# A new order for a planned attention and convolution kernel: other due times, other engines for some eighty steps

## The chip, the cores and the metric

The kernel runs on one core of a Trainium2 chip. A core has TensorE (PE; its weight loads are counted apart as PEld), VectorE (DVE), ScalarE (ACT), GpSimd (POOL) and SyncE (SP), which here only starts DMAs; 16 DMA engines serve all its queues. The metric is the device time of one execution in microseconds (us). The three runs of the kernel before took 371.64, 371.68 and 374.29, so the median is 371.68.

## The reference

Four batches of eight heads, 768 positions, 64 channels a head. First comes attention in which a query sees only the keys of its own cluster:

```python
q_assign = np.argmax(np.einsum('bhsd,hcd->bhsc', q_n, c_n), axis=-1)   # 16 centroids a head
k_assign = np.argmax(np.einsum('bhsd,hcd->bhsc', k_n, c_n), axis=-1)
mask = q_assign[:, :, :, None] == k_assign[:, :, None, :]
scores = np.where(mask, scale * np.matmul(q, k.transpose(0, 1, 3, 2)), -1000000000.0)
attn = softmax(scores)
out = np.matmul(attn, v)
```

The eight heads of a batch are put side by side to 512 columns, x, and a gated long convolution follows:

```python
proj = x @ w_proj                                  # 512 -> 3 * 512: x1, x2, x3
X2 = np.fft.rfft(x2, n=S, axis=1)
H = np.fft.rfft(filter_fft, n=S, axis=0)[None, :, :]
y = x1 * np.fft.irfft(X2 * H, n=S, axis=1) * x3
return (y @ w_out).astype(np.float32)
```

## The kernel before, in words

**Units.** The work is cut into eight groups `n` (half a batch, four heads each), and each group into two pairs of heads. For a pair, `attention` (line 683 on) runs over six tiles of 128 keys. For each tile there are three score products of 512 columns (`sc`, line 700), three exponentials on ACT into a buffer `p` (lines 714 and 717), the product p·V (`pv`, line 728, 96 of them in all, numbered 1 to 96 in this document), and the sum of the p for the softmax's denominator: the first two tiles are added by DVE or POOL (line 737), the other four by DVE (line 741). There are five buffers `p`.

**Masks.** A query and a key of different clusters must give a score far below the others. Keys and queries carry 16 more rows for that beside their 64 channels in the tiles `aug`: the one-hot of the cluster, for queries scaled and shifted. `routing` (line 589 on) makes them for a group: products with the centroids (`L647`), a transposition and an argmax on DVE (`L652` to `L662`), two products with a triangular matrix that pick the first of equal maxima (`bank<-ohB,tri`, one for each half of the positions), two small steps for each of them on ACT or DVE that write `ohT` (`L673` or `L675`), and then eight DMAs of 24 KB (`aug<-ohT`, line 512), which put the rows where the score products read them.

**Loads.** Queries, keys and V come by DMA from SP's queue (lines 324, 331, 337, 343). Keys of the later groups come in four pieces and are transposed by DVE (`L605`), queries are transposed by PE (`L627`). A load can begin when the step that last read its buffer is done. There are four buffers for queries and keys and three for V. The filter (line 432, into `y`) and the weights (lines 1097 and 1101, POOL's queue) are loaded once.

**Denominators.** For most pairs the sum over partitions is made by DMAs: three accumulating moves from POOL's queue (`acc<-acc`, line 774), a move to DRAM (`dd<-acc`, line 778), and from there back, a reduction and a reciprocal on DVE (`dn`, `L787`), and two broadcasting loads (`rb<-dr`, line 791). For the first two and the last groups PE makes it with a product with ones (`L754`) and one copy (`den`, `L760` or `L762`).

**Convolution.** When both groups of a batch are done, `hyena` runs beside the attention of the next: products with w_proj (`L855` for x2; the gate products `bank<-xT,wpj` for x1 and x3), forward transform, products with the filter's spectrum `hm` on DVE (`L885`), inverse transform (`bank<-inv,y`), folding (`L956`, `L966`), gating (`L929`, `L971`) and the product with w_out.

**What sets the order.** No order of instructions is written down. Every step is recorded with `op`, line 95: the engines that may run it with a cost for each, its reads and writes, and a due time. `place`, line 124, then runs a list planner on these costs: whenever an engine is free, it takes, among the steps that can start within 0.1, the one with the smallest due time, and for a step with several engines the engine that can start it first. Loads (`kind="load"`) don't start before their due time, on SP's queue as on POOL's. The steps are then issued in the order of their planned starts, and each engine runs its own part of that list in order; SP and POOL, too, do not pass a DMA that waits. Two tables adjust the planner, both keyed by the running number of the step:

```python
o.due += NUDGE.get(o.seq, 0.0)
```

```python
if o.seq in ONLY:
    o.eng = {ONLY[o.seq]: o.eng[ONLY[o.seq]]}
```

`NUDGE` (line 43) has an entry for each of the 1983 steps and is added to its due time. `ONLY` (line 44) fixes the engine of some steps. PE has two more details: a product of 128 output rows is issued as one instruction when the array stands in its mode of 128 columns and as two of 64 columns otherwise (`product`, line 80), and score products and gate products take the mode that they find.

Of the kernel before, what the change touches and what calls it, by code (L numbers as in the profile page):

```python
# [87 lines left out]
class Plan:  # L88
# [6 lines left out]
    def op(self, eng, fn, due, r=(), w=(), alloc=None, free=(), lock=False, byts=0, after=(), kind=None, lat=0.0, tab=None):  # L95
# [3 lines left out]
        o.seq = len(self.ops)  # L99
        o.due += NUDGE.get(o.seq, 0.0)  # L100
        o.outs, o.end, o.start, o.on = [], None, None, None
# [22 lines left out]
    def place(self, free0, banks_for, switch=0.1, wait=0.1, rate=RATE, bonus=0.0, margin=0.02195, shape=0.0):  # L124
# [58 lines left out]
        for o in self.ops:  # L183
            if o.seq in ONLY:
                o.eng = {ONLY[o.seq]: o.eng[ONLY[o.seq]]}
        for o in self.ops:
# [1109 lines left out]
```

## Time and profile before

| | us |
|---|---|
| median of three runs | 371.68 |
| the profiled execution | 372.84 |
| its span | 371.1 |
| PE busy in the span | 354.5 |
| DVE busy | 337.6 |
| ACT busy | 264.3 |
| POOL busy | 121.5 |

The span is from the first to the last instruction in the profile; 1.74 us of the execution's time lie around it. PE's busy time holds matmuls only, and their ends are modelled. The longest groups are the 768 instructions of p·V with 142.7 us and the exponentials with 109.1 and 57.9 us; DVE spends 111.9 us in the sums of line 741. Where a view names what an engine waited for, it takes the last of the semaphores that the instruction waited on.

### The profile page before, as it was taken

The page shows a single profiled execution, that of the slowest core. Times are in us where ns is not written, and L with a number is a line of the kernel's source. Part 1 is how long each engine was busy: PE and PEld are TensorE (multiplying, and loading weights), DVE is VectorE, ACT ScalarE, POOL GpSimd, SP SyncE. Part 2 cuts the span into 40 slices and gives each one's busy share as a digit, 9 for nine tenths or more (in the row PEclk, how much of TensorE's full clock was granted, in tenths as well). Part 3 has the DMA queues.
Part 4 walks back from the last instruction along what each step waited for, and adds up shares of the span by engine and source line. Part 5 has one row for each costly group of instructions (what it writes and reads, how often), then busy time and mean ns, then how long its engine had stood idle before and what let it go on. Part 6 is the DMA issues. An engine that isn't in the chain of part 4 may idle for free.

```text
span 371.1 us, 8436 instructions
## 1 busy us (share of the span) xinstructions
PE 354.5 (96%) x3191; PEld 202.5 (55%) x3191; DVE 337.6 (91%) x449; ACT 264.3 (71%) x502; POOL 121.5 (33%) x152
## 2 busy tenths in 40 slices
PE   7999989999999999999989999968999999999995
PEld 4555445444555554654546545545466766566662
DVE  6988887999999879999998999998998999989993
ACT  7999977876977686797798673758965787323433
POOL 7452442300035447123100057425021432134610
PEclk9999999999999999999999999999999999999999
DMA  7879897364599866769667958673367650110214
GB/s 173 214 147 202 174 175 168 76 136 76 120 182 171 139 118 100 118 149 140 119 85 167 241 108 127 146 137 41 88 97 184 147 76 0 47 45 2 116 57 172
DMA packets 109797, 46.20 MB, mean 124 GB/s; under 512 B 97640, under 2 KB 103484, under 8 KB 109756
## 3 DMA queue, kind: packets, MB, share of 16 engines
q1 hardware_dynamic: 105772, 36.05, 43.1%
q0 software_dynamic: 2752, 8.98, 17.1%
q10 hardware_dynamic: 1232, 0.62, 0.6%
q8 instruction: 25, 0.41, 0.5%
q14 instruction: 16, 0.13, 0.1%
HBM read 31.59 MB, written 7.40 MB: 105 GB/s over the span
## 4 chain that ended last, share of the span: by engine, by line
PE 56%; DVE 21%; ACT 6%; DMA 6%; issue 5%; POOL 2%; SPq 2%; DVEq 0%; ACTq 0%; POOLq 0%
PE bank L85 23%; PE pair L728 23%; DVE acc L741 5%; DMA qkraw<-in_k_dram 2%; PE bank L855 2%; DVE xT L820 2%; PE bank L83 2%; PE bank L627 2%; PE bank L647 2%; DVE sd L956 2%; DVE tm L869 1%; DMA aug<-ohT 1%; DVE acc L737 1%; DMA dd<-acc 1%; DVE yy L966 1%
## 5 line engine op out<-in xcount | busy, mean ns | idle before, releaser
L728 PE MATMUL pair<-p,vraw 128*64 128x385 f32 x768 | 142.7, 488 | 0.8 <-ACT p L717 0.8
L717 ACT ACTIVATE p<-bank 128x512 f32<-128x512 f32 x192 | 109.1, 612 | 19.0 <-PE bank L85 10.7
L741 DVE TENSOR_TENSOR acc<-p,acc 128x1536 f32<-128x1536 f32 x64 | 111.9, 1749 | 4.3 <-POOL acc L737 1.6
L728 PEld LDWEIGHTS pair<-p,vraw 128*64 128x64 f32 x768 | 56.2, 136 | 45.9 <-issue 38.1
L85 PE MATMUL bank<-aug,aug 80*64 80x256 bf16 (+3 forms) x682 | 75.5, 327 | 4.2 <-DMA aug<-ohT 1.4
L85 PEld LDWEIGHTS <-aug 80*64 80x64 bf16 (+1 forms) x682 | 42.4, 109 | 41.4 <-issue 29.6
L714 ACT ACTIVATE p<-bank 128x512 f32<-128x512 f32 x96 | 57.9, 607 | 7.5 <-PE bank L85 6.2
L774 POOL DMA_DIRECT2D acc<-acc x30 | 24.0, 819 | 102.5 <-DVE acc L741 46.6
L85 PE MATMUL bank<-xT,wpj 128*64 128x384 bf16 x488 | 44.8, 326 | 1.2 <-ACT ohT L673 1.1
L285 POOL CAST aug<-qkP 64x768 bf16<-64x768 f32 x26 | 21.3, 823 | 66.1 <-DVE acc L741 23.3
L85 PEld LDWEIGHTS <-wpj 128*64 128x64 bf16 x488 | 30.3, 110 | 13.3 <-issue 4.3
L85 PEld LDWEIGHTS <-y 128*64 128x64 bf16 x456 | 23.9, 110 | 14.6 <-issue 5.1
L885 DVE TENSOR_TENSOR tm<-bank,hm 128x512 f32<-128x512 f32 x44 | 28.5, 682 | 3.0 <-PE bank L490 2.0
L85 PE MATMUL bank<-wout,y 128*64 128x512 bf16 (+1 forms) x200 | 24.2, 372 | 1.3 <-DVE y L971 0.9
L889 POOL TENSOR_TENSOR y<-tm 128x512 bf16<-128x512 f32 x16 | 20.2, 1274 | 14.0 <-DVE tm L885 7.7
L737 POOL TENSOR_TENSOR acc<-p,p 128x1536 f32<-128x1536 f32 x6 | 20.7, 3458 | 8.7 <-DVE uv L874 4.4
L283 ACT COPY qkP<-bank 128x384 f32<-128x384 f32 x35 | 15.8, 480 | 10.0 <-PE bank L85 4.6
L855 PE MATMUL bank<-wpj,xT 128*64 128x512 bf16 x192 | 22.0, 379 | 0.2 <-DVE xT L820 0.2
L283 ACT COPY ob<-bank 128x512 f32<-128x512 f32 x22 | 12.4, 594 | 13.4 <-PE bank L85 9.9
L283 ACT CAST aug<-qkP 64x768 bf16<-64x768 f32 x25 | 20.5, 829 | 0.4
L737 DVE TENSOR_TENSOR acc<-p,p 128x1536 f32<-128x1536 f32 x10 | 17.7, 1765 | 2.9 <-ACT p L714 1.4
L627 PE MATMUL bank<-ident,qkraw 128*128 128x128 f32 x120 | 18.6, 281 | 0.8 <-DMA qkraw<-in_k_dram 0.8
(176 smaller groups left out, 443.1 us busy)
## 6 DMA issues: line engine op xcount, KB each, us to landing
qkraw<-in_q_dram SPq DMA_DIRECT2D x30, 192.0 KB, 3.4
rb<-dr SPq DMA_DIRECT2D x30, 192.0 KB, 3.3
qkraw<-in_k_dram SPq DMA_DIRECT2D x50, 96.0 KB, 2.8
vraw<-in_v_dram SPq DMA_DIRECT2D x48, 96.0 KB, 3.1
out_dram<-ob SPq DMA_DIRECT2D x9, 512.0 KB, 3.1
acc<-acc POOLq DMA_DIRECT2D x10, 384.0 KB, 5.1
acc<-acc POOLq DMA_DIRECT2D x10, 192.0 KB, 4.2
vraw<-in_v_dram SPq DMA_DIRECT2D x4, 384.0 KB, 4.3
```

The costliest lines, as they stand in the source:

```text
L85: T.nc.tensor.matmul(out[64 * i:64 * i + 64], lhsT[:, 64 * i:64 * i + 64], rhs, start=start, stop=stop)
L283: T.nc.scalar.copy(out, in_)
L285: (T.nc.vector if e == "DVE" else T.nc.gpsimd).tensor_copy(out, in_)
L627: T.nc.tensor.transpose(ap(h)[:, ts(t, 128)], raw(s, 3 * ch + t), T.ident[:, ::-1] if ch > j else T.ident)
L714: T.nc.scalar.activation(o, ap(h).rearrange("p (a b) -> p a b", a=2), Act.Exp, scale=0.125)
L717: T.nc.scalar.activation(flat(s)[:, lo:lo + 512], ap(h), Act.Exp, scale=0.125)
L728: T.nc.tensor.matmul(o[64 * hp:64 * hp + 64, ch, :385], T.vraw[vs][:, hp, sk * D:(sk + 1) * D], T.p[slots[sk]][:, hp, 384 * ch:384 * ch + ...
L737: alu(e).tensor_tensor(T.acc[os], T.p[slots[0]][:, :, :S], T.p[slots[1]][:, :, :S], op=Alu.add)
L741: T.nc.vector.tensor_tensor(T.acc[os], T.p[slots[sk]][:, :, :S], T.acc[os], op=Alu.add)
L774: op(("POOL", .8), lambda e, rows=rows: T.nc.gpsimd.dma_start(flat_()[:rows], flat_()[rows:2 * rows], accum_op=Alu.add), te, r=[], w=AK, b ...
L855: T.nc.tensor.matmul(ap(h)[64 * i:64 * i + 64], T.xT[xs][:, kt, c:c + 64], T.wpj[:, kt, DM:2 * DM], start=kt == 0, stop=kt == ND - 1)
L885: op(("DVE", .68), lambda e, i=i, cs=cs, r=r, h=h: T.nc.vector.tensor_tensor(T.tm[r][:, cs], ap(h), hmrow(i, (0, 2, 2, 3)[2 * r + cs]), op ...
```

## The change

Only the two tables change. All 1983 entries of `NUDGE` are new numbers. `ONLY` has 102 entries where it had 113. Cut to entries that are spoken of, each on a line of its own:

```diff
-NUDGE = {
+NUDGE = {
...
-128:-20.837, 129:-31.203, 130:-22.135, 131:21.705,        # filter loads
+128:13.22, 129:12.796, 130:-10.311, 131:10.695,
...
-266:-49.0695, 267:15.6865, 268:11.6885, 269:13.0825,      # four pieces of keys, group 2, first pair
+266:-4.39, 267:4.93, 268:0.957, 269:8.02,
...
-684:-14.97122,                                            # dd<-acc, group 2, first pair
+684:-2.473,
...
-1196:-842.80587, 1197:-916.07187, 1198:-711.43587, 1199:-834.24287,   # masks, group 5
+1196:-19.574, 1197:-42.2, 1198:-17.755, 1199:-21.803,
...
-1338:8.27978, 1339:16.77478, 1340:12.95378, 1341:6.79878, # four pieces of V, group 6, first pair
+1338:-8.792, 1339:-8.067, 1340:-9.3, 1341:-2.232,
...
-1366:-212.95227, 1369:-4591.25327,                        # bank<-ohB,tri of group 6, two halves
+1366:0.062, 1369:1.656,
...
...
-ONLY = {
+ONLY = {
...
-72:"ACT", 149:"ACT", 224:"POOL", 231:"POOL", 252:"ACT", 255:"ACT",
+72:"DVE", 149:"DVE", 155:"DVE", 176:"DVE", 224:"DVE", 231:"DVE", 252:"DVE", 255:"DVE",
...
```

A due time says nothing by itself: it counts against those of the other steps that are ready. What comes out in the order of the instructions is this. PE has the same 634 groups of products, in nearly the same order for score products and p·V; the others move by some places against them. 15 score products instead of 32 find the array in the mode of 128 columns, so PE has 2284 matmuls instead of 2267 to issue, for the same columns. Of the 48 loads of V pieces 29 stand earlier against PE's work and 16 later, 8 groups of products earlier in the mean; of the 48 of key pieces 35 earlier and 9 later, 4 groups in the mean. The 60 mask moves stand as before in the mean, 29 earlier and 24 later. The V pieces of group 6's first pair are issued when products 64 to 67 stand next to them in the list, before 70 to 72; they are first needed by product 73. Of the key pieces of group 2's first pair three stand 14, 11 and 3 groups earlier, one 5 later.

Some eighty steps change their engine. Counted by engine, DVE has one cast to `aug` more, two output copies, two scalings `tm<-bank,hw` (line 468) and two denominators more, one step `L405` and one copy to `fw` more, one `ohT` and two copies `x` more, three copies to `qkP`, one `od` and one `L966` less. ACT has the most of these the other way and three casts and three `qkP` copies more. POOL has four casts and one fill less and one fold more. Of the first sums p + p (line 737) that of group 0's first pair goes from POOL to DVE and that of group 1's second pair from DVE to POOL. On DVE, two of the products into `hm` stand ahead of the first transposition of keys, where all stood behind it.

More of the change, by code (lines that the diff above doesn't have):

```diff
@@ new lines @@
+ONLY = {15:"POOL",16:"ACT",17:"POOL",30:"ACT",32:"SP",33:"SP",34:"SP",35:"SP",37:"SP",38:"SP",40:"SP",67:"ACT",69:"DVE",72:"DVE",73:"DVE",86:"DVE",91:"DVE",100:"POOL",101:"POOL",147:"ACT",149:"DVE",155:"DVE",159:"DVE",161:"DVE",176:"DVE",224:"DVE",225:"POOL",230:"DVE",231:"DVE",236:"POOL",237:"DVE",243:"DVE",251:"DVE",252:"DVE",254:"ACT",255:"DVE",325:"ACT",408:"POOL",411:"POOL",418:"POOL",420:"ACT",421:"POOL",503:"ACT",526:"ACT",531:"DVE",532:"DVE",533:"POOL",563:"DVE",571:"POOL",600:"DVE",701:"POOL",703:"POOL",706:"ACT",708:"ACT",710:"POOL",712:"DVE",873:"DVE",876:"ACT",879:"ACT",880:"POOL",884:"DVE",889:"POOL",901:"DVE",1033:"DVE",1042:"DVE",1071:"DVE",1072:"POOL",1085:"POOL",1087:"DVE",1096:"ACT",1099:"ACT",1167:"DVE",1169:"ACT",1171:"POOL",1174:"POOL",1179:"ACT",1183:"POOL",1355:"ACT",1356:"POOL",1358:"POOL",1461:"DVE",1489:"POOL",1529:"ACT",1533:"DVE",1537:"ACT",1555:"POOL",1641:"ACT",1644:"POOL",1649:"ACT",1650:"ACT",1843:"DVE",1911:"POOL",1919:"ACT",1960:"SP",1963:"SP",1966:"ACT",1969:"DVE",1970:"SP",1974:"SP",1977:"ACT",1978:"ACT",1981:"ACT"}
```

3 lines of the change are left out of this document (1 added, 2 removed).

## The prediction

> **What bounds the kernel now.** I read the busy shares first, then the same in stretches, then the waits of PE, then the instructions in order of time where PE stood still.
>
> ```profile
> PE 354.5 (96%) x3191; PEld 202.5 (55%) x3191; DVE 337.6 (91%) x449; ACT 264.3 (71%) x502; POOL 121.5 (33%) x152
> ...
> 0.00:10.00 10.00, 8.12 (x39) 4.60 (x39) 6.90 (x25) 7.44 (x12) 7.17 (x40) 1.00 0.74 167
> 10.00:25.00 15.00, 13.86 (x128) 7.67 (x128) 14.01 (x28) 14.63 (x31) 7.98 (x17) 1.00 0.80 167
> 25.00:60.00 35.00, 33.78 (x270) 18.14 (x268) 27.88 (x24) 31.38 (x62) 14.44 (x12) 1.00 0.92 185
> 60.00:120.00 60.00, 59.73 (x491) 30.57 (x490) 58.55 (x60) 47.67 (x93) 10.65 (x14) 1.00 0.64 132
> 120.00:240.00 120.00, 117.16 (x1001) 64.35 (x999) 112.37 (x145) 88.92 (x166) 42.28 (x39) 1.00 0.74 134
> 240.00:255.00 15.00, 10.99 (x144) 8.30 (x142) 13.03 (x22) 8.96 (x19) 5.19 (x5) 1.00 0.64 120
> 255.00:360.00 105.00, 104.81 (x1083) 66.11 (x1079) 99.63 (x140) 61.42 (x119) 33.78 (x26) 1.00 0.32 72
> 360.00:371.10 11.10, 6.10 (x56) 2.78 (x54) 5.25 (x11) 3.86 (x8) 0.00 (x0) 0.95 0.50 190
> ```
>
> A row of the stretches gives the stretch and its length, busy time of PE, PEld, DVE, ACT and POOL, the granted clock, the DMA share and GB/s. PE is the engine to count by: its clock is full (1.00) in every stretch but the last, and what it has to compute isn't changed. It stands still for 3.0 us before 25 (1.88 + 1.14, the head) and 5.0 after 360 (the last products and output). Between them it idles 1.22 + 0.27 up to 120, 2.84 up to 240, 4.01 in the fifteen microseconds after 240 and 0.19 up to 360: 8.5 us in all. This is the most that a better order can gain from PE's waits, 2.3%. DVE is the second bound: 58.55 of 60 us between 60 and 120, but only 27.88 of 35 before that.
>
> Where the 8.5 us lie, in slices of five and in the waits of PE:
>
> ```profile
> 50.00:55.00 5.00, 3.81 (x32) 1.80 (x30) 3.58 (x5) 3.33 (x7) 3.62 (x3) 1.00 0.74 159
> ...
> 130.00:135.00 5.00, 4.25 (x36) 2.09 (x32) 2.65 (x3) 3.99 (x7) 4.15 (x2) 1.00 0.86 147
> 190.00:195.00 5.00, 3.79 (x33) 1.96 (x34) 4.90 (x9) 4.96 (x9) 0.00 (x0) 1.00 0.46 64
> ...
> PE bank L85 <- ACT ohT L673: 2.2, 2, 1.1
> PE bank L85 <- DMA aug<-ohT: 1.4, 2, 1.0
> PE bank L85 <- DVE hm L470: 1.2, 1, 1.2
> ```
>
> **Part 1, keys of group 2 (50 to 55).** The wait of 1.2 us on `hm` is the second end of a late load:
>
> ```profile
> 41.86 5.69 SPq L324 DMA_DIRECT2D qkraw<-in_k_dram  x3
> ...
> 43.91 8.66 DMA qkraw<-in_k_dram
> ...
> 52.76 0.98 DVE L605 STREAM_TRANSPOSE qkP<-qkraw 128x768 f32<-128x768 f32 x1 [1.39 <-DMA qkraw<-in_k_dram]
> ```
>
> Three of the four pieces of that key pair are issued from 41.86 on, the one that ends last lands 8.66 us after its issue, DVE stands still 1.39 us before its transposition, and the `hm` products that PE needs stand behind the transposition. In the changed order those three pieces stand 14, 11 and 3 groups of PE work further ahead, two `hm` instructions stand in front of the transposition, and the last of the four filter loads, which shares the queue, is sooner by one product p·V. Either of the first two takes the 1.19 us that PE lost in this slice; beyond that nothing is gained here, since DVE then ends last. I take -1.2, between 0 and -1.4 (DVE's own wait).
>
> **Part 2, group 6 (240 to 255).** In order of time:
>
> ```profile
> 242.44 0.47 ACT L283 COPY x<-bank 128x384 f32<-128x384 f32 x1
> 242.96 0.35 PE L85 MATMUL bank<-ohB,tri 128*64 128x384 bf16 x2 [0.83 <-ACT x L283]
> 243.35 1.00 ACT L673 ACTIVATE ohT<-bank 64x384 bf16<-64x384 f32 x2 [0.44 <-PE bank L85]
> 244.39 0.35 PE L85 MATMUL bank<-ohB,tri 128*64 128x384 bf16 x2 [1.08 <-ACT ohT L673]
> ...
> 245.29 6.80 SPq L512 DMA_DIRECT2D aug<-ohT  x8
> 245.83 4.74 PE L85 MATMUL bank<-xT,wpj 128*64 128x384 bf16 x56 [1.08 <-ACT ohT L673]
> 251.58 0.41 PE L85 MATMUL bank<-aug,aug 80*64 80x512 bf16 x2 [1.01 <-DMA aug<-ohT]
> ```
>
> Four waits make up the 4.0 us: 0.83, 1.08, 1.08, 1.01. Before, the two products of the one-hot rows (`ohB,tri`) stand directly behind one another, so the second and the next product each wait for a bank until ACT has done both copies of the one before (1.00 us). In the changed order a gate product stands between the two halves (eight times two instructions, 4.74 / 56 x 8 = 0.68 us), and the first half stands ahead of the gate copy `x` that ended the first wait. That should remove 0.83 and about 0.68 of each 1.08: 2.2. Against it, the copy `x` (0.47) now stands on ACT between the two pairs of `ohT` copies, so the masks' moves start relative to PE's work no sooner, and the last wait (1.01) stays: seven gate products stand ahead of the first score product in both orders. The four pieces of V of group 6 stand at the products 64 to 67 instead of 70 to 72, the last of them just ahead of these rows. No row shows PE waiting for them, so this counts nothing by itself; it takes a transfer out of the way of the masks. I take -2.0, between +0.5 (the copy `x` passes into the mask chain) and -4.0 (all four waits go).
>
> **Part 3, masks of group 5 and the sum of group 3.** The second row of `aug<-ohT` above belongs to 190 to 195: 1.4 less 1.01 is 0.4. There the masks stand one product sooner: -0.4, between 0 and -0.4; the rest of the 1.21 idle there has another cause and stays. At 130:
>
> ```profile
> 130.15 3.45 POOL L737 TENSOR_TENSOR acc<-p,p 128x1536 f32<-128x1536 f32 x1 [1.39 <-DMA dd<-acc]
> ```
>
> The sum of the first two p on POOL is held 1.39 us until the older sum has been moved out; PE lost 0.75 us in that slice. The move out stands ahead of one more product in the changed order: -0.4, between 0 and -0.75.
>
> **Part 4, work that changes engine.** About 80 elementwise steps do. In the head, where ACT is busy 14.63 of 15 us from 10 to 25, it ends with about one step less (0.5 us each, by the row at 243.35) and one more DMA issue; I call that zero, between -0.6 and +0.6. For DVE over the whole kernel:
>
> ```profile
> L285 DVE CAST aug<-qkP 64x768 bf16<-64x768 f32 x13 | 7.5, 579 | 0.3
> ...
> L285 DVE COPY qkP<-bank 128x384 f32<-128x384 f32 x13 | 6.7, 548 | 0.5 <-PE bank L627 0.2
> ...
> L398 DVE SCALAR_TENSOR_TENSOR tm<-x,s0t,ob 128x384 f32<-128x384 f32 x3 | 1.9, 639 | 0.1
> ...
> L285 DVE COPY tm<-bank 128x512 f32<-128x512 f32 x1 | 0.7, 692 | 0.3 <-PE bank L855 0.3
> ```
>
> One cast to `aug` more (0.58), two copies and two scalings of 512 columns more (4 x 0.69), one three-operand step more (0.64), and of the steps of 384 columns, all near 0.55, one more on balance: +4.5 us of DVE work. Two sums p + p change places between DVE and POOL, which cancels. Nearly all of the rest stands ahead of product 20, so before 80 us. What is ahead of 60 is covered by the 7.1 us that DVE stands still between 25 and 60. Behind that, DVE has 1.45 us of slack in 60, and about 0.6 us more work net (a scaling, a copy, a cast and a denominator come, a sum of 1.75 goes). I take +0.5, between 0 and +4.5 (no cover at all).
>
> **Part 5, new waits.** Nearly every instruction moves against another engine's by a place or two. The old order has waits of PE, up to 1.2 us each in the rows above, that nobody put there; a new one will have some where this one has none. I allow +0.5, between 0 and +4.
>
> The sum: -1.2 - 2.0 - 0.4 - 0.4 + 0.5 + 0.5 = **-3.0 us**. The profiled execution took 372.84 (span 371.1 and 1.74 around it), so it would take 369.8; it lies 1.16 above the median of the runs shown, and the median goes from 371.68 to **368.7**. A change of under 1%, 3.7 us, is about what a measurement of this kernel can't tell from none.
>
> **Rivals.** *All of it comes.* The four places at their far ends, -1.4 - 4.0 - 0.4 - 0.75, and nothing given back: -6.5, 365.2. For it: each of these waits is at one spot, and the order was changed at each. Against it: part 2's last wait has the same seven products as cover.
>
> *The loads are not what is late, the DMA engines are.* Then a piece that is begun sooner only lands when the others let it, and part 1 and the masks give nothing.
>
> ```profile
> aug<-ohT SPq DMA_DIRECT2D x60, 24.0 KB, 2.2
> ```
>
> For it: the DMA share is 0.92 between 25 and 60, one key piece took 8.66 us to land, and the mask after 245 landed over 5 us after its issue where the median is 2.2. Against it: after 60 the share is 0.64 to 0.74, so there is room. The price: part 2's bank waits still go, perhaps half (-1.0), the DVE work comes (+0.5), new waits (+0.5): 371.7. The Trainium skill, "DMA: Bandwidth & Descriptors", section "Issuing engines are not separate DMA queues", says that transfers run on the same 16 engines and interleave whichever engine began them; by that rule alone this rival holds before 60 us, and the trace agrees with its 0.92 there; it does not speak against the later places.
>
> *DVE takes over.* The 4.5 us find no cover, because the pieces that come sooner also let DVE's long sums start sooner and the 7.1 us of slack before 60 were only the other side of the waits that go. This decides from the point where DVE's share before 60 is as high as between 60 and 120 (98%): then each added microsecond is one of the span, and the waits that went come back as waits for DVE: 371.7 + 4.5 = 376.2. For it: the 98%. Against it: most of the added steps stand where DVE idles 20% of the time.
>
> **How the numbers follow.** The forecast (367 to 371) 0.46; all of it 0.18; DMA the limit (370.7 to 372.7) 0.20; DVE takes over, or new waits of the same price, 0.16. Faster by over 1% means under 368.0: all of the second case and some four tenths of the first, 0.37. Slower by over 1% means above 375.4: most of the last case, 0.14. Within 1%: 0.49. The range reaches from 363.5, part 2 and the rest gone with some of ACT's head as well, to 374.5, where half of the last case is left out.
>
> **What would show it.** Right: in the fifteen microseconds around group 6's masks PE stands still 2 us rather than 4, with no row of `ohB,tri` waiting for `ohT`; no `L605` waits for a key near 52; DVE's busy total is 342. Wrong: key pieces landing after 8 us as before; DVE above 95% from 25 to 60 with PE waiting for `hm`, `aug` or `acc`; a new wait of more than 2 us at a place where this trace has none, above all a mask or a V piece that waits on SP behind a `dn` or `dd` step.

## The result, and the profile after

The changed kernel takes **369.85 us** (median of 12 runs, 368.66 to 371.61); the kernel before took 373.56 in runs beside it. The ratio is **0.9903, 95% interval 0.9881 to 0.9925**: about 1% less time, at the edge of what was called measurable. The profiled execution took 370.38 us, with a span of 368.7; before it was 372.84 and 371.1. The forecast for it was 369.8, from a sum of -3.0; it came to -2.46. The medians, which are over all executions, lie 3.7 apart; the ratios leave out the few executions that were over 1.5% longer than the fastest of the same kernel. The sum was near. Its terms were not: the largest was too small, one did not come, one was missed, and loads that stand sooner work otherwise than was assumed.

The same stretches as before, changed kernel (stretch and length, then busy time of PE, PEld, DVE, ACT and POOL, the granted clock, DMA share, GB/s):

```profile
0.00:10.00 10.00, 8.23 (x32) 4.12 (x32) 6.31 (x21) 5.39 (x10) 6.55 (x37) 1.00 0.75 169
10.00:25.00 15.00, 12.91 (x120) 7.60 (x120) 14.36 (x32) 14.73 (x30) 6.83 (x18) 1.00 0.78 183
25.00:60.00 35.00, 34.05 (x275) 18.43 (x275) 31.63 (x29) 31.13 (x60) 11.17 (x9) 1.00 0.88 164
60.00:120.00 60.00, 59.24 (x495) 32.14 (x489) 58.01 (x61) 48.03 (x94) 12.05 (x13) 1.00 0.65 136
120.00:240.00 120.00, 119.09 (x1028) 66.90 (x1028) 114.37 (x149) 90.94 (x169) 44.63 (x42) 1.00 0.78 142
240.00:255.00 15.00, 13.77 (x163) 9.89 (x161) 14.35 (x23) 10.69 (x23) 6.82 (x7) 1.00 0.56 87
255.00:360.00 105.00, 103.75 (x1067) 62.06 (x1065) 99.60 (x141) 59.80 (x116) 31.20 (x25) 1.00 0.33 76
360.00:368.70 8.70, 4.51 (x48) 2.19 (x42) 3.57 (x7) 2.83 (x6) 0.00 (x0) 1.00 0.48 181
```

PE's idle time, before and after: 240 to 255, 4.01 and 1.23; 120 to 240, 2.84 and 0.91. These two stretches gain 4.7 us. Against them, 10 to 25 has 1.14 and 2.09, 60 to 120 has 0.27 and 0.76, and 255 to the end has 5.19 and 5.44. Over the whole span PE idles 13.1 instead of 16.6.

What PE waits for, changed kernel (total us, times, longest):

```profile
PE bank L85 <- DVE hm L470: 0.9, 2, 0.5
PE bank L85 <- ACT ohT L673: 0.9, 2, 0.7
PE bank L527 <- POOL aug L285: 0.8, 1, 0.8
...
PE bank L368 <- DVE sd L365: 0.6, 1, 0.6
PE bank L537 <- ACT sim L283: 0.6, 1, 0.6
```

The wait for `aug<-ohT` (1.4 before) is gone and the one for `ohT` has fallen from 2.2 to 0.9. The wait for `hm` is still there, in two pieces, and the last three rows lie in the head, between 9 and 16 us: two of them are new, the one for `sim` was 0.3 before.

**Group 6**, changed kernel, in order of time:

```profile
242.86 0.35 PE L85 MATMUL bank<-ohB,tri 128*64 128x384 bf16 x2 [0.68 <-ACT ohT L673]
243.33 0.99 ACT L673 ACTIVATE ohT<-bank 64x384 bf16<-64x384 f32 x2
...
243.84 5.24 SPq L512 DMA_DIRECT2D aug<-ohT  x6
...
244.38 4.11 PE L85 MATMUL bank<-xT,wpj 128*64 128x384 bf16 x48 [0.18 <-ACT ohT L673]
...
248.61 0.41 PE L85 MATMUL bank<-aug,aug 80*64 80x512 bf16 x2
```

The waits of 0.83, 1.08 and 1.08 have become 0.68 and 0.18. The first mask move is issued at 243.84 instead of 245.29, and the first score product, at 248.61, waits for nothing.

**Keys of group 2.** The wait at 52 moved to 57:

```profile
44.86 2.13 POOL L1097 DMA_DIRECT2D wpj<-in_moe_w_proj_dram  x4 [0.31 <-POOL wpj L1094]
...
45.26 0.60 SPq L324 DMA_DIRECT2D qkraw<-in_k_dram  x1
...
55.49 0.41 PE L85 MATMUL bank<-aug,aug 80*64 80x256 bf16 x4 [0.53 <-DVE hm L470]
...
57.84 0.98 DVE L605 STREAM_TRANSPOSE qkP<-qkraw 128x768 f32<-128x768 f32 x1 [1.75 <-DMA qkraw<-in_k_dram]
```

and the chain of waits has for that load (start, duration until it landed):

```profile
45.26 12.55 DMA qkraw<-in_k_dram
```

The last key piece is issued 0.4 us behind the first of the four loads of `w_proj`, 384 KB each, and takes 12.55 us to land; in the kernel before, the piece that landed last took 8.66. Between 50 and 70 PE loses 1.34 us; before it lost 1.19, all of it between 50 and 55.

**The head**, ACT's queue in the changed kernel, and the square root of line 357 in the kernel before:

```profile
3.94 0.83 ACT L1081 ACTIVATE aug<-ident 64x768 bf16<-64x768 f32 x1
6.98 0.40 ACTq L331 DMA_DIRECT2D qkraw<-in_k_dram  x1
7.43 0.85 ACT L1081 ACTIVATE aug<-ident 64x768 bf16<-64x768 f32 x1 [2.66 <-DMA qkraw<-in_q_dram]
...
8.18 0.19 ACT L357 ACTIVATE s<-ss 128x1 f32<-128x1 f32 x1
```

```profile
5.81 0.19 ACT L357 ACTIVATE s<-ss 128x1 f32<-128x1 f32 x1
```

ACT issues a load behind its first fill, and the load is held from 4.77 to 6.98 until another load has landed; the square root behind it comes 2.4 us later, and with it the centroids and the first products of the routing. Why it is held is seen in the compiled program: the DMAs of SP's and ACT's queues take eight semaphores in turn, and from the ninth on each waits until the eighth before it has landed. This load is the fourteenth and waits for the sixth, a load of queries, as the row at 7.43 has it. From the first rows of ACT's part of the program, changed kernel:

```
2 L331 DMACopy qkraw_93<-in_k_dram 128x6x64
...
7 L331 DMACopy qkraw_91<-in_k_dram 128x3x64 [waits DMAHW5_49]
...
9 L357 Activation s_76<-ss 128x1 [waits DVE_49]
```

In the kernel before, ACT issued its two loads of keys among the first eight; those of the head that wait all stood on SP, where only other DMAs are behind them.

### The profile page after: what moved, and what is told of

Its sections match the earlier page's. It is cut to its first block, busy times and chain, and to the rows that moved or that the text cites. A ratio compares the mean times of both kernels' runs of the same rounds, so it can differ in the third digit from the quotient of the medians.

```text
span 368.7 us, 8460 instructions
## 1 busy us (share of the span) xinstructions
PE 355.6 (96%) x3205; PEld 203.3 (55%) x3208; DVE 342.2 (93%) x456; ACT 263.5 (71%) x499; POOL 119.2 (32%) x148
## 4 chain that ended last, share of the span: by engine, by line
PE 63%; DVE 12%; DMA 9%; ACT 7%; SPq 5%; issue 2%; ACTq 0%; DVEq 0%
PE bank L85 27%; PE pair L728 24%; PE bank L855 6%; DVE acc L741 4%; DMA qkraw<-in_k_dram 3%; ACT p L717 3%; DMA rb<-dr 3%; SPq L512 2%; PE bank L647 2%; PE bank L627 2%; SPq L331 1%; DMA aug<-ohT 1%; ACT p L714 1%; DMA qkraw<-in_q_dram 1%; PE bank L83 1%
## 5 line engine op out<-in xcount | busy, mean ns | idle before, releaser
L85 PE MATMUL bank<-aug,aug 128*64 128x256 bf16 (+3 forms) x728 | 82.5, 327 | 2.3 <-DVE hm L470 0.9
L728 PEld LDWEIGHTS pair<-p,vraw 128*64 128x64 f32 x768 | 57.1, 136 | 47.2 <-issue 37.0
L85 PEld LDWEIGHTS <-aug 80*64 80x64 bf16 (+1 forms) x728 | 46.0, 109 | 40.1 <-issue 27.2
L85 PE MATMUL bank<-xT,wpj 128*64 128x384 bf16 x480 | 45.8, 326 | 0.3 <-ACT ohT L673 0.2
L285 POOL CAST aug<-qkP 64x768 bf16<-64x768 f32 x22 | 19.6, 892 | 75.5 <-DVE acc L741 47.4
L283 ACT CAST aug<-qkP 64x768 bf16<-64x768 f32 x28 | 23.0, 829 | 5.5 <-DVE qkP L605 3.4
L283 ACT COPY qkP<-bank 128x384 f32<-128x384 f32 x38 | 17.5, 484 | 9.0 <-PE bank L85 5.7
L627 PEld LDWEIGHTS bank<-ident,qkraw 128*128 128x128 f32 x120 | 13.6, 144 | 8.8 <-issue 4.3
```

The source lines that it names most:

```text
L85: T.nc.tensor.matmul(out[64 * i:64 * i + 64], lhsT[:, 64 * i:64 * i + 64], rhs, start=start, stop=stop)
L283: T.nc.scalar.copy(out, in_)
L627: T.nc.tensor.transpose(ap(h)[:, ts(t, 128)], raw(s, 3 * ch + t), T.ident[:, ::-1] if ch > j else T.ident)
L728: T.nc.tensor.matmul(o[64 * hp:64 * hp + 64, ch, :385], T.vraw[vs][:, hp, sk * D:(sk + 1) * D], T.p[slots[sk]][:, hp, 384 * ch:384 * ch + ...
```

## The experiments

In the diffs, `b` and `a` are the planned lists of steps with their engines, before and changed; q["ACT"] is one engine's part of such a list. All kernels compute the whole reference.

| run | what it is | median us | ratio to before, 95% | span |
|---|---|---|---|---|
| changed kernel | | 369.85 | 0.9903 (0.9881 to 0.9925) | 368.7 |
| b1_a | head of before, then changed | 367.87 | 0.9865 (0.9815 to 0.9914) | 365.0 |
| b20_a | before to product 20, then changed | 372.60 | 0.9987 (0.9954 to 1.0020) | 370.2 |
| b66_a | before to product 66, then changed | 373.07 | 1.0014 (0.9979 to 1.0049) | 373.1 |
| b_gate | before, group 6's products in an order like the changed one | 374.05 | 1.0016 (0.9976 to 1.0056) | 380.8 |
| a_root | changed, square root first | 370.44 | 0.9924 (0.9895 to 0.9953) | 371.1 |
| a_wproj_late | changed, w_proj later | 369.03 | 0.9886 (0.9850 to 0.9922) | 367.0 |
| a_keys_first | changed, key pieces sooner | 371.60 | 0.9942 (0.9910 to 0.9974) | 370.5 |
| a_sp_old | changed, SP's order of before | 381.17 | 1.0205 (1.0160 to 1.0250) | 378.2 |
| a_ungate | changed, group 6's products as before | 370.96 | 0.9944 (0.9913 to 0.9976) | 367.4 |
| a_first_loads | changed, first twelve loads as before | 368.40 | 0.9853 (0.9828 to 0.9878) | 366.1 |
| b_sp_new | before, SP's order of the change | 381.23 | 1.0216 (1.0180 to 1.0253) | 379.7 |
| b1_a_ohT | b1_a and two edits on ACT | 367.51 | 0.9844 (0.9812 to 0.9877) | 366.8 |

### Cuts: do the stretches add up?

```diff
-order = a
+order = b up to product k, then the steps that are left in the order of a      # k = 1, 20, 66
```

> The order before up to product 1 (the head), the changed order from there. Theory (the four stretches add up, each with the idle time of PE that the two profiles show: head +0.84 lost, 25 to 120 about +0.2 lost, 120 to 240 -1.93, 240 to 255 -2.78, the end +0.3): the head's 0.84 comes back, so the span is 0.8 below that of the changed kernel, 367.9, and the ratio to the kernel before 0.988 where the changed kernel has 0.990. Rival (the head's loss is made up later anyway, because DVE or the DMA engines set the time up to 60): no difference to the changed kernel, 368.7.

> The order before up to product 20 (about 80 us), the changed order from there: this leaves out all that the change does to the keys of group 2, the head, and nearly all steps that change engine. Theory (stretches add up): only the gains behind 120 us are left, -1.93 - 2.78 + 0.3 = -4.4, and the span is 366.7. Rival (the work that left DVE, ACT and POOL early and the earlier loads are what the later gains rest on): less than -1.5, span above 369.6.

> The order before up to product 66, the changed order from there: this keeps the changed order of group 6's masks, products and most of its V loads. Theory (stretches add up): -2.8 from 240 to 255, +0.3 at the end, span 368.6. Rival (the gains of 120 to 240 and of 240 to 255 are one gain, an earlier start of the same chain): -1 or less, span above 370.

**b1_a**: span 365.0, more than the 0.8 expected. The first output copy `osb` starts at 36.57 instead of 38.13, so the head alone is 1.56, and the third is 3.46 sooner; from there on the distance stays between 2.9 and 3.8. **b20_a and b66_a** were both slower than the theory by 3.5 to 4.5 us; their medians are 0.7 and 0.3 us below that of the kernel before in runs beside them, 373.32. The rows of the places say that the gains are there: group 6's waits are 0.68 and 0.18 in both, as in the changed kernel. What eats them stands behind the cut. b20_a:

```profile
80.70 0.52 PE L85 MATMUL bank<-ohB,tri 128*64 128x384 bf16 x4 [0.89 <-DVE ohB L662]
...
91.07 0.52 PE L85 MATMUL bank<-aug,aug 80*64 80x512 bf16 x4 [1.89 <-DMA aug<-ohT]
92.21 1.61 PE L85 MATMUL bank<-aug,aug 128*64 128x256 bf16 x18 [0.63 <-DMA aug<-ohT]
```

and in b66_a a wait of 1.68 for `xT` at 208.78. PE idles 4.3 us between 75 and 95 in b20_a and 0.2 before. So group 6's gain is there without the rest, but these two orders could not be joined in the middle without a cost of about the size of the gains: such a cut doesn't measure a stretch.

### The head

> The changed kernel with one instruction moved: on ACT, the square root for the centroids' norm (line 357) stands ahead of the load of queries or keys that ACT's queue issues third, where the change put it behind that load and one fill. Theory (the head's loss is this one step: ACT stands still 2.66 us at the load, from 4.77 to 7.43, and the square root starts at 8.18 where it started at 5.81 before): it starts near 5, PE's wait of 0.65 for sd and most of 0.79 + 0.59 behind it go, PE idles 3.0 us before 25 instead of 3.86, and with the later start of everything behind it the span falls by 1.0 to 1.6, to 367.1 to 367.7. If the lateness of the head is also what makes the key pieces of group 2 late, another 1 to 1.9 goes and the span is near 365.5. Rival (the load itself is what is late, not the root): PE waits for the transposition of that load instead, span 368.7 within 0.4.

```diff
-q["ACT"]: ..., fill aug, load (third), fill aug, square root L357, ...
+q["ACT"]: ..., fill aug, square root L357, load (third), fill aug, ...
```

The first theory fell, and the rival holds. In a_root, ACT's load and PE behind it:

```profile
4.99 0.20 ACT L357 ACTIVATE s<-ss 128x1 f32<-128x1 f32 x1 [0.23 <-DVE ss L356]
7.44 0.40 ACTq L331 DMA_DIRECT2D qkraw<-in_k_dram  x1
...
10.83 0.52 PE L627 MATMUL bank<-ident,qkraw 128*128 128x128 f32 x3 [1.34 <-DMA qkraw<-in_k_dram]
```

The root is at 4.99 as expected, but the load now goes at 7.44, and PE waits for its keys. PE idles 4.38 us before 25, no less than the 3.86 of the changed kernel. The load was itself urgent, and being the fourteenth it can't go before the sixth has landed. So the second try gives the head the first twelve loads of the kernel before:

> The changed kernel with the first twelve loads of group 0's queries and keys on the engines and in the order of the kernel before: ACT issues two of them at its start and none behind its fills, SP the other ten. Nothing else of the head is put back. Theory (the head's loss is the load that ACT's queue holds from 4.77 to 6.98 until another load has landed): the square root of line 357 starts near 5, no wait of PE over 1 before 20 us, PE idles 3.0 before 25, span 1.0 to 1.6 less, 367.1 to 367.7, and near 365.5 if the sooner filter loads also take the wait for keys near 57. Rival (the head's loss is the elementwise work that went to DVE and ACT there): PE idles 3.7 or more before 25, span within 0.5 of 368.7.

```diff
-q["ACT"]: centroids, key load 39, ..., fill, key load 36, fill, root, ..., query load 30, ...
+q["ACT"]: centroids, key load 33, key load 35, ..., fills, root, ...
-q["SP"]:  35, 40, 38, 37, 33, 29, 32, 34, 31, ...
+q["SP"]:  40, 39, 37, 38, 34, 36, 30, 29, 32, 31, ...
```

The root starts at 5.79 and PE idles 2.68 us before 25:

```profile
8.90 0.30 PE L368 MATMUL bank<-ident,sd 128*64 128x128 f32 x1 [0.24 <-DVE sd L365]
10.82 1.80 PE L527 MATMUL bank<-qkP,cbd 128*32 128x384 f32 x12 [0.54 <-POOL aug L285]
```

The span is 366.1, and the interval of the ratio, 0.9828 to 0.9878, lies wholly below that of the changed kernel. Five loads on other engines and an order of twelve are worth 1.5 us by the medians and 2 by the ratios; the elementwise work that the change moved in the head is left as changed and costs nothing that shows.

### Keys: a late issue, or full DMA engines?

> The changed kernel with the four loads of w_proj on POOL's queue put behind the cast near 55 us; they were issued from 44.86 on, 0.4 us ahead of the last key piece of group 2's first pair, which took 12.55 us to land. Theory (the DMA engines are what is late there): the piece lands within 5 us of its issue near 45, the L605 row near 57 has no wait for keys (1.75 before), PE's waits of 0.53, 0.15, 0.38 for hm and h between 55 and 62 go, 0.5 to 1.9 gained, span 366.8 to 368.2, less what the later flood of w_proj costs the loads of 55 to 70. Rival (the piece is late because it is issued late on SP): it still takes over 9 us and nothing is gained.

> The changed kernel with the last two key pieces of group 2's first pair put ahead of the third and fourth filter load on SP, so that they are issued near 37 instead of 40.8 and 45.26. Theory that a sooner issue is what counts: they land before 50, the wait of L605 near 57 goes, 0.5 to 1.9 gained, span 366.8 to 368.2. Rival (the DMA engines are full there and the order only shifts the lateness): the filter loads, the four loads of w_proj that wait for them and the mask moves come later by what the keys came sooner, and the span is 368.7 within 0.5.

```diff
 # a_wproj_late
-q["POOL"]: 334, w_proj 337, 338, 335, 336, cast 408, ...
+q["POOL"]: 334, cast 408, w_proj 337, 338, 335, 336, ...
 # a_keys_first
-q["SP"]: ..., filter 129, 128, keys 268, mask, query, keys 267, 2 masks, keys 269, ...
+q["SP"]: ..., keys 267, 269, filter 129, 128, keys 268, mask, query, 2 masks, ...
```

With `w_proj` out of its way the key piece is there in time: it landed 2.55 us after its issue, and DVE's row at 56.53 waits for no key. In a_keys_first the wait is gone too. Neither gives PE its time back. a_wproj_late, and then a_keys_first, where the second row is a new wait further on:

```profile
56.00 0.41 PE L85 MATMUL bank<-aug,aug 80*64 80x256 bf16 x4 [1.11 <-DVE hm L470]
...
56.53 0.96 DVE L605 STREAM_TRANSPOSE qkP<-qkraw 128x768 f32<-128x768 f32 x1
```

```profile
56.37 0.41 PE L85 MATMUL bank<-aug,aug 80*64 80x256 bf16 x4 [0.72 <-DVE hm L470]
...
161.99 1.55 PE L85 MATMUL bank<-aug,aug 80*64 80x256 bf16 x14 [1.42 <-DVE x L929]
```

Between 50 and 70 PE idles 1.14 and 1.05 us, against 1.34 in the changed kernel. The time of a_wproj_late can't be told from that of the changed kernel (0.9886 and 0.9903, the intervals overlap), and a_keys_first is no faster either (0.9942). The first shows what made the piece late; both show that the lateness isn't all that PE waits for, since `hm` is late on DVE without it.

When a load has landed is recorded too: a DMA here tells it by sixteen updates of its semaphore. The last of these, with the times of issue, for the last key piece of that pair and for `w_proj`:

| kernel | w_proj issued | last w_proj landed | key piece issued | key piece landed |
|---|---|---|---|---|
| changed kernel | 44.86 to 46.43 | 57.59 | 45.26 | 57.82 |
| a_root | 45.23 to 46.81 | 56.75 | 45.66 | 56.99 |
| a_first_loads | 43.28 to 44.86 | 54.60 | 43.65 | 54.85 |
| b1_a | 41.48 to 43.05 | 53.05 | 43.15 | 53.23 |
| a_ungate | 44.65 to 46.22 | 57.25 | 44.64 | 49.98 |
| a_wproj_late | from 53.62 | after 56 | 45.60 | 48.15 |

Issued behind the first load of `w_proj`, the piece lands 0.2 to 0.3 us behind the last of the four. In a_ungate, below, whose order is that of the changed kernel up to 235 us, it was issued at the same moment as the first and landed 5.3 us later; DVE waits for no key there, and PE lost only 0.41 between 50 and 70. So 0.4 us in the issue went with 7.8 in the landing, and a_wproj_late, where only `w_proj` was moved, shows the same. In the kernel before, three of the four loads were issued from 41.00 to 42.10, and three key pieces landed 0.3, 0.8 and 1.2 us behind the third. What PE loses at this place still differs by some 0.7 us between executions in which DVE waits for no key, and with one profile of each kernel such differences, b1_a's second 1.9 among them, aren't settled.

### SP's queue: are sooner loads the gain?

> The changed kernel with SP's queue in the order of the kernel before, all other engines as changed: loads and moves of masks are no longer begun sooner against one another. Theory (the gain is the order of PE and ACT at single places, and the loads have room behind 60 us): the span stays within 1 of 368.7. Rival (the change is what its name says, and the sooner loads and mask moves make the gain): the masks and keys come late again, waits of PE for aug<-ohT and of DVE for qkraw return, and all of the 2.4 us are lost, span 371 or more.

> The kernel before with SP's queue in the order of the changed kernel, nothing else: the loads and mask moves are begun sooner against one another, the steps of all other engines stand as before. Theory (an order of SP fits only the order of the other engines that it was made with): slower, 2 us or more, span above 373. Rival (loads and moves begun sooner are worth something by themselves): the waits for keys at 52 and for masks at 192 and 251 go, 0.5 to 2 gained, span 369.1 to 370.6.

```diff
 # a_sp_old
-q["SP"] = SP's steps in the order of a
+q["SP"] = SP's steps in the order of b          # all else as a; b_sp_new: the other way round
```

Both lose: a_sp_old takes 381.17, 3% more than the changed kernel (9.5 us in the span), and b_sp_new 2.2% more than the kernel before (8.6 us in the span). The old order in the changed kernel, near 90 us:

```profile
83.85 0.55 SPq L766 DMA_DIRECT2D dd<-den  x1
...
84.50 3.79 SPq L512 DMA_DIRECT2D aug<-ohT  x6
...
88.38 0.59 SPq L768 DMA_DIRECT2D dn<-dd  x1
...
90.48 0.23 DVE L787 RECIPROCAL dn<-dn 128x12 f32<-128x12 f32 x1 [4.91 <-DMA dn<-dd]
...
92.38 1.51 PE L754 MATMUL bank<-acc,ones 128*32 128x384 f32 x8 [4.80 <-DVE acc L741]
```

The denominator's way back from DRAM stands on SP behind six mask moves; DVE stands still 4.91 us for it, and PE 4.80. The new order in the kernel before loses as much in its own places:

```profile
84.75 0.52 PE L627 MATMUL bank<-ident,qkraw 128*128 128x128 f32 x3 [3.60 <-DMA qkraw<-in_q_dram]
...
95.87 2.98 PE L85 MATMUL bank<-aug,aug 128*64 128x256 bf16 x18 [3.06 <-DMA aug<-ohT]
```

So neither order of SP is better by itself, as the theory of b_sp_new had it: of these two, each fits the order of the engines that it was planned with. The theory of a_sp_old, that SP's order hardly matters behind 60 us, is wrong by 9 us.

### Group 6: products or masks?

> The kernel before with two steps moved: the gate product that followed the two halves of bank<-ohB,tri of group 6 stands between them, and the copy x that stood ahead of the first two ohT copies stands behind all four. Nothing is changed in the loads. Theory (the waits for banks are the cost): the waits of 0.83 and 1.08 + 1.08 shrink to about 0.8 together; the masks start about 1 sooner, PE comes to the first score product 2.2 sooner, so the wait for them grows from 1.0 to about 2.2, and 1.0 to 2.0 are gained, span 369.1 to 370.1. Rival (the masks' way is the limit, and only the loads that the change takes out of their way shorten it): the wait for the masks grows by all that is gained, -0.3 or less.

> The changed kernel with only group 6's two steps put back: the two halves of bank<-ohB,tri stand directly behind one another, the gate product ahead of them, and on ACT the copy x ahead of the first ohT copies. Loads and moves as changed. Theory (the order of these products and copies is what gained there): the waits of 0.83 and 1.08 + 1.08 come back in place of 0.68 + 0.18, 1.4 to 2.1 lost, span 370.1 to 370.8. Rival (what gained there are the mask moves, which start sooner because the loads were taken out of their way): 0.5 or less lost, and no wait for masks.

```diff
 # b_gate, from the kernel before
-q["PE"]:  gate product, half, half, gate product
+q["PE"]:  gate product, half, gate product, half
-q["ACT"]: copy x, ohT, ohT, ohT, ohT
+q["ACT"]: ohT, ohT, copy x, ohT, ohT
 # a_ungate, from the changed kernel
-q["PE"]:  first half, gate product, second half, gate product
+q["PE"]:  gate product, first half, second half, gate product
-q["ACT"]: ohT, ohT, copy x, ohT, ohT
+q["ACT"]: copy x, ohT, ohT, ohT, ohT
```

b_gate is not quite what was announced, nor the order of the change: the copy `x` stands between the two pairs of `ohT` copies, not behind all four, and between the halves stands the gate product that followed them, where the change has the one that stood ahead of them. Its profiled execution ran at a granted clock of 0.982 and waited 4.32 us for a load near 50, so only the rows at the place are read: waits of 1.67 for the copy `x`, 0.75 for `sd` and 0.51 for masks, 2.9 in all where there were 4.0. The place gained 1.1 and the time, 1.0016, shows nothing of it: inconclusive. a_ungate shows more:

```profile
241.25 0.35 PE L85 MATMUL bank<-ohB,tri 128*64 128x384 bf16 x2 [1.29 <-ACT ohT L673]
242.69 4.09 PE L85 MATMUL bank<-xT,wpj 128*64 128x384 bf16 x48 [0.43 <-ACT ohT L673]
247.65 0.41 PE L85 MATMUL bank<-aug,aug 80*64 80x512 bf16 x2 [0.87 <-DVE sd L956]
```

PE is busy 17.31 us between 235 and 255 where it was 18.68: 1.4 is lost at the place by two moved steps, 0.9 of it in waits for `ohT`. The ratio, 0.9944 against 0.9903, points the same way, though the intervals overlap; the span of the profiled execution, 367.4, does not: PE idles 0.6 us more than in the changed kernel, but its busy total is 1.9 less, and that total differs between executions. The row at 247.65 names `sd`, but this product also waits for the first two mask moves, by the compiled program, and the second of them had landed only at 247.51, and `sd` ended at 247.54: with PE done at 246.78, the masks alone would have held it 0.7 us. The two runs with exchanged SP orders have the same question. a_sp_old has the changed products with the old loads, b_sp_new the old products with the changed loads; the last fence is a stretch of b_sp_new, in the columns of the table of stretches:

```profile
251.71 0.35 PE L85 MATMUL bank<-ohB,tri 128*64 128x384 bf16 x2 [0.68 <-ACT ohT L673]
...
258.39 0.41 PE L85 MATMUL bank<-aug,aug 80*64 80x512 bf16 x2 [1.06 <-DMA aug<-ohT]
```

```profile
252.62 0.35 PE L85 MATMUL bank<-ohB,tri 128*64 128x384 bf16 x2 [1.08 <-ACT ohT L673]
254.04 6.28 PE L85 MATMUL bank<-xT,wpj 128*64 128x384 bf16 x56 [1.07 <-ACT ohT L673]
260.13 0.41 PE L85 MATMUL bank<-aug,aug 80*64 80x512 bf16 x2
```

```profile
255.00:258.00 3.00, 3.00 (x26) 2.23 (x24) 2.33 (x4) 0.48 (x1) 0.00 (x0) 0.63 0.81 154
```

The waits for `ohT` follow the order of the products, whichever order SP has. For the wait for masks no such sentence holds. b_sp_new has none, but its granted clock was 0.63 from 255 to 258, and the 56 instructions ahead of the score product took 6.28 us instead of 4.74, time that the masks had. From the issue of the first mask move to the landing of the second it is 6.25 us in the kernel before, 5.16 in a_sp_old and 5.06 in b_gate, with SP's old order; with the new one it is 4.64 in the changed kernel and from 2.45 to 5.36, the last in a_ungate, over eleven kernels. So that way is mostly shorter with the new order, but not so much that the wait is gone whatever PE does: a_first_loads still waits 0.31 for masks. Of the place's gain, about 2 is the products' (0.9 to 1.4 where they are put back alone); how much of the last 1.0 is due to SP's order isn't settled.

### A version that beats both

> The order before up to product 1, the changed order from there, and two edits on ACT: near 240 the copies od, x and osb stand behind the first two, or all four, ohT copies, and near 263 the copy osb stands one exponential sooner. Theory: the first ohT copies start 0.3 sooner and with them the second half's product and the masks, so that 0.3 to 0.7 of the waits 0.69, 0.18 and 0.38 go, and the wait of 0.48 for osb goes: span 363.8 to 364.3 where the version without these edits had 365.0. Rival (the waits for banks move to the copies that were put back): span 365.0 or more.

```diff
 # on ACT, on top of b1_a
-osb, od, ohT, ohT, x, ohT, ohT          (group 6)
+ohT, ohT, od, ohT, ohT, x, osb
-exp 1690, exp 1677, osb 1620            (near 263)
+exp 1677, osb 1620, exp 1690
```

The wait for `osb` is gone. At group 6 the rival holds:

```profile
240.92 0.35 PE L85 MATMUL bank<-ohB,tri 128*64 128x384 bf16 x2 [0.43 <-ACT ohT L673]
242.44 2.79 PE L85 MATMUL bank<-xT,wpj 128*64 128x384 bf16 x32 [1.17 <-ACT ohT L673]
245.43 2.14 PE L85 MATMUL bank<-xT,wpj 128*64 128x384 bf16 x24 [0.20 <-ACT x L283]
```

1.80 for banks where b1_a has 0.69 + 0.18 for banks and 0.38 for masks: the copies that were put back hold banks. The time, 367.51, can't be told from b1_a's 367.87. This version and a_first_loads are about 0.5% faster than the changed kernel; b1_a's interval overlaps with that of the changed kernel.

## Why the prediction was right, and where not

By its own parts, in PE's idle time unless said otherwise:

| part | forecast | measured |
|---|---|---|
| 1, keys of group 2 | -1.2 | +0.15 (50 to 70) |
| 2, group 6 | -2.0 | -2.8 |
| 3, masks of group 5 and the sum at 130 | -0.8 | -1.6 |
| 4, head | 0 | +1.05 (up to 30) |
| 4, work on DVE | +0.5 | not seen apart |
| 5, new waits | +0.5 | +0.47 (265 to 270) |
| not foreseen, 200 to 220 | | -0.7 |

**Part 1 failed in the profiled execution.** The step that failed is that a piece which stands 14, 11 or 3 groups sooner is also begun and landed sooner. It held for two of the three: issued at 38.81 and 40.79 instead of 41.86 and 43.91, ahead of `w_proj`, they landed at 45.68 and 46.90 instead of 51.67 and 52.56, and the wait at 52 went. The third stood 3 groups further ahead but behind two mask moves that took SP from 41.55 to 45.22, so it was issued at 45.26 instead of 42.53, fell behind the first load of `w_proj`, and the wait came back at 57 as 1.75. In a_ungate, with the same order, the piece was issued together with that load, and the place idles 0.41: -0.8 came there, so the +0.15 in the table is partly chance. The rival "the DMA engines are what is late" described this place. By the Trainium skill's "DMA: Bandwidth & Descriptors", section "Issuing engines are not separate DMA queues", transfers of all queues interleave on the same 16 engines, and the trace agrees: from 50 to 54 us it has 259 packets of 3072 bytes from POOL's queue and 314 of 128 bytes from SP's, about one for one, so that `w_proj` moved 777 KB and the key piece 39. The sign of error named in advance, a key piece that lands after 8 us, is what came.

**Part 2 was right in its mechanism, and its size was off in one term.** The gate product between the halves and the copy `x` behind the first `ohT` copies took 2.1 of 2.99 (0.83 + 1.08 + 1.08 to 0.68 + 0.18), where 2.2 was worked out; a_ungate brings 0.9 of it back. One sign of being right did not come: a row of `ohB,tri` still waits for `ohT`, 0.68. The wait for masks, 1.01, was said to stay, and V's four pieces at products 64 to 67 were counted as nothing "by itself". That step failed: the score product at 248.61 waits for nothing, since the second mask move landed at 248.48, just when PE was done with the gate products. That SP's order did it is likely, but not shown: with that order the wait is 0 in the changed kernel and 0.31 in a_first_loads, and in a_ungate the masks alone would have made it 0.7. Which of SP's moves matter, V's pieces or others, wasn't tried either.

**Part 3 was under-sized.** 190 to 195 idles 0.39 instead of 1.21, and 130 to 135 nothing instead of 0.75: both at their far ends or beyond. Of the 1.21, 0.41 was the wait for masks and 0.80 one for an exponential, which was said to stay and fell to 0.29. No run takes these places apart, so why they gained stays open.

**Part 4 missed the head.** It counted steps and "one more DMA issue" on ACT as zero, between -0.6 and +0.6. The step that failed is the price of that issue: not the 0.4 us of the instruction, but the 2.2 us that it is held, with the square root behind it. On DVE the forecast of 342 came out at 342.2, and the cover held: DVE is busy 31.63 of 35 from 25 to 60, 90%, below the 95% at which its rival was to begin. Only at `hm` near 56, in the two runs without the wait for keys, PE waits for DVE with no other cause seen.

**Part 5** was an allowance, and that one new wait, for `osb` at 266, came to 0.47 is luck. The gain from 200 to 220 (the waits of 0.24 for `xT` and 0.40 for `uv` are gone) came unforeseen; no run isolates it.

PE's idle time fell by 3.5 and the span by 2.4. The difference is PE's busy total, 355.6 and 354.5 before; its ends are modelled, and it lies between 353.7 and 357.0 in the profiled executions of the nine kernels that show 3205 to 3208 matmuls. So the terms above aren't good to better than 1 us in sum. The total was right partly by luck, because the errors had both signs: without the head's loss the forecast would have been 2 us too high, as a_first_loads shows (367.93 against 369.8).

## What to carry to other kernels

An order of loads can't be judged by how much sooner each load is begun: in this program each one is held by the eighth before it, so moving one load holds others, and the order of loads that stands in the faster kernel costs 2% beside the other order of the engines. What counted for the load of small packets was the large load beside it: issued with the first load of `w_proj` it took 5.3 us to land, 0.4 us behind it 12.55. Keep loads off a compute engine's queue once that many are under way; the price is not the issue but what stands behind it. And when an order is changed as a whole, exchange one queue at a time in both directions: that showed that neither order of the queue is better by itself, which cutting the order in time did not.

## What the runs showed that was not expected

A load on ACT's queue stood 2.2 us (4.77 to 6.98) before it was issued, and the fills and the root behind it with it. The same key piece took 9.3 to 12.6 us to land in the executions of five kernels where it was issued behind the first load of `w_proj`, and 5.3 where it was issued together with it, against a median of 3.3 for such pieces: packets of 128 bytes took turns with packets of 3072. And 2 to 3% of the time, two to three times the whole effect of the change, hang on the order of one queue that computes nothing.
